# One more buffer for queries and keys, nine weight pieces and another order of mish ahead of an attention and mixture-of-experts kernel

## The chip, the cores and the metric

The kernel runs on one core of a Trainium2 chip. The time is device time in microseconds (us) of one execution; three executions of the kernel before took 829.11, 832.15 and 832.38 us, so the median is 832.15. One further execution was profiled; all rows of this document that show the kernel before come from it.

The core has TensorE (PE in the rows; PEld is its loading of weights), VectorE (DVE), ScalarE (ACT) and GpSimd (POOL). SP and ScalarE each have a queue from which they start DMA transfers (SPq, ACTq).

## The reference

Three parts follow one another on 2304 tokens:

```python
# attention: q, k, v are [4, 8, 576, 64]; heads 0-3 window 32, heads 4-7 window 128 with step 4
attn = softmax(where(mask, q @ k.T / 8, -1e9));  x = attn @ v        # x: [2304, 512]
# dense layer with mish
h = x @ w_in                                                        # [2304, 2048]
x = (h * tanh(softplus(h))) @ w_out                                  # [2304, 512]
# eight experts, one per token
e = argmax(x @ w_gate);  p = softmax(x @ w_gate)[e];  s = sigmoid(x @ w_output_gate)[e]
out = p * s * (relu(x @ w1[e]) @ w2[e])                              # w1: 512x1024, w2: 1024x512
```

## The kernel before

**Halves and tasks.** The tokens are worked in NH = 8 half-batches j of 288 tokens. The attention of a half-batch is four tasks (j, p), each a pair of heads: p = 0, 1 have the plain window, p = 2, 3 the dilated one. `load(j, p)` (line 202) brings what a task needs, queries, keys and values side by side, in one transfer into one tile `qkv` (992 or 1216 columns; line 213). Tasks of j = 0, 1 load on SP into memory that weights take later. The tasks from j = 2 on load on ScalarE's queue and share two buffers, so the load of task t + 2 can start when the last reader of task t, its product with the values (`o`, line 315), is done. A task is then: scores (`sc`, line 251), a row maximum on VectorE, exponentials on ScalarE (line 278), a division by the sums, transposes (`tp`, line 295) and the product `o`, which is split into two parts `xhi`, `xlo` (lines 325, 328).

**The dense layer.** Every product runs in three passes over a high and a low part of both factors (high times high, high times low, low times high). A step g of the main loop handles 128 of the 2048 hidden columns for one half-batch: `l1` (line 494) makes `hps` with 12 matmuls; mish is computed in place in a tile `e` by steps a to d; `l2` (line 547) adds its product with `w_out` to `acc`, three steps later. The steps of mish are: a1 an exponential on ScalarE that reads `hps` (line 502), a2 a minimum and an addition on VectorE (line 505), a3 a square on ScalarE (line 510), b a logarithm and an exponential on ScalarE (lines 522, 523), c a product with `hps` on VectorE (line 528), d the split into `ghi` on ScalarE (line 417) and `glo` on VectorE (line 418). `hps` has two buffers, so `l1` of step g + 2 has to wait for c of step g.

**Weights.** The weights of the dense layer come in 32 pieces of 128 x 512 values, alternately of `w_in` and `w_out`. SP loads a piece into a staging tile `wst`; it is narrowed to the bits that a matmul uses in two steps (`upper`, line 401 on ScalarE or 403 on VectorE, then `wf`, line 407 on VectorE) and split into a high part on ScalarE (line 448 or 417) and a low part on VectorE (line 453 or 418).

**Order.** `ahead` is the front of the program: in it the order on TensorE, ScalarE, VectorE and SP is as written. Its iterations t carry one task of j = 0, 1 each in a pipeline (scores of t + 1, exponentials of t, transposes and `o` of t - 1, split of t - 2); beside it the first seven pieces (`wide_first`, line 163) are narrowed, cast on ScalarE, and the first four `l1` steps with their mish are run. After `ahead` a scheduler orders by priority. The main loop calls l1, mish and l2 and spreads the attention of the next half-batch over its steps; `att_d` of a task (its `o`) is followed by `next_load`, the load of the task two further on.

**The end.** The experts run one after another on rows gathered by expert. The outputs of the last expert are two row tiles; each goes through ScalarE or, for every second tile, half through VectorE and half through ScalarE, and is then scattered to `out` by an indirect DMA of GpSimd (line 908). A count of tokens that didn't fit (`rest_count`) is read into a register of every engine, and a loop `rest` runs that often, which is zero times for these inputs.

Of the kernel before, what the change touches and what calls it, by code (L numbers as in the profile page):

```python
# [9 lines left out]
F32 = mybir.dt.float32  # L10
# [13 lines left out]
DIL = 4  # L24
# [7 lines left out]
def tile_attn_mish_moe(ctx, tc, qkv, w_in, w_out, w_gate, w_og, w1, w2, out):  # L32
# [108 lines left out]

    def setup_rows(e):
        if not fills:
            fills.append(mp.tile([128, ROW], F32, tag="fill", name="fill", bufs=1))
            nc.vector.memset(fills[0], 0.0)
            nc.gpsimd.iota(fills[0].bitcast(I32)[:, DM + 1:DM + 2], pattern=[[0, 1]], base=OOB, channel_multiplier=1)
        for i in range(0, MOST, 128 * (MOST // 128)):
            n = min(128 * (MOST // 128), MOST - i)
            k, m = max(1, n // 128), min(n, 128)
            tc.keep_in_program_order(nc.sync.dma_start(  # L150
                out=buf[e * NT + i:e * NT + i + n, :].rearrange("(i p) c -> p i c", p=m),
                in_=fills[0][0:m].unsqueeze(1).to_broadcast([m, k, ROW])))
# [7 lines left out]
        xlo[j] = xp.tile([128, KD, HS], F32R, tag="xlo", name="xlo")  # L160

    EARLY = 2
    wide_first = 7
    STEPS = 4
    LAG = 3
    AHEAD = 3
# [38 lines left out]
    def load(j, p):  # L205

        n = 992 if p < 2 else 1216
        if j < 2 and p:
            off = 992 + 1216 * (p - 2) if p > 1 else 0
            t = scq[j][:, off:off + n]  # L210
        else:
            t = raw.tile([128, 1216], F32, tag="qkv", name="qkv", bufs=2)[:, 0:n]
        (nc.sync if j < 2 else nc.scalar).dma_start(out=t, in_=qkv[j, p, :, 0:n])
        kv = t[:, HS:]
        if p < 2:
            kT, vr = kv[:, 0:HS + 32], kv[:, HS + 32:].rearrange("p (u h d) -> p u h d", u=3, h=2)
        else:
            kT = kv[:, 0:HS + 4 * 32].rearrange("d (c p) -> d c p", c=DIL)
            vr = kv[:, HS + 4 * 32:].rearrange("p (h c d) -> p h c d", h=2, c=DIL)
        state[j, p] = dict(qT=t[:, 0:HS], kT=kT, v=vr)  # L220

    def form(j, p):
        return (3, CH, 128) if p < 2 else (DIL, NP, NP + 32 * (j % 2))
# [129 lines left out]
    def next_load():  # L353
        if n_l[0] < len(tasks):
            load(*tasks[n_l[0]])
            n_l[0] += 1

    def attention(j):

        ops = []  # L360
        for p in range(5):
            if p < 4:
                ops.append(lambda p=p: att_s(j, p))
            if p > 0:
                ops.append(lambda p=p: att_c(j, p - 1))
                ops.append(lambda p=p: (att_d(j, p - 1), next_load()))
        return ops


# [498 lines left out]
    def e_l2_end(q, part):  # L868

        for t, (i, m) in enumerate(part):  # L870
            for f in (NF2 - 2, NF2 - 1):
                for n, (a, x) in enumerate(PASS):
                    nc.tensor.matmul(out=accs["e", q][t], lhsT=gt["e", q, f][x][:, i:i + m],
                                     rhs=ew[q, 1, a][:, DM * f:DM * f + DM], start=False, stop=(f == NF2 - 1 and n == 2))
            e_row(q, i, m, accs["e", q][t], t)

    def e_l2(q, f, part):

        gg = gt.pop(("e", q, f))
# [18 lines left out]
    def e_row(q, i, m, src, alt=0):  # L898

        x = meta[q, 0][0:m, i // 128, :]  # L900
        o = rp.tile([128, DM], F32, tag="row", name="eo")
        if alt % 2:

            nc.vector.tensor_scalar(out=o[0:m, 0:DM // 2], in0=src[:, 0:DM // 2], scalar1=x[:, 0:1], scalar2=None, op0=ALU.mult)
            nc.scalar.activation(out=o[0:m, DM // 2:], in_=src[:, DM // 2:], func=AF.Copy, scale=x[:, 0:1])
        else:
            nc.scalar.activation(out=o[0:m], in_=src, func=AF.Copy, scale=x[:, 0:1])
# [27 lines left out]
    def rest_count():  # L935
# [21 lines left out]
        return cnt, rem, nc.values_load(tn[0:1, 0:1], min_val=0, max_val=NT // 128 + E)  # L957

    def rest(cnt, rem, n):

# [65 lines left out]
    def ahead(load_w, warm):  # L1026
# [12 lines left out]
            a_max(*t, 0)  # L1039
            a_max(*t, 1)  # L1040
        last = None
        for t in range(len(T) + 2):
            now = T[t] if t < len(T) else None
            old = T[t - 1] if 0 < t <= len(T) else None
            old2 = T[t - 2] if 1 < t else None
            new = T[t + 1] if 0 < t < len(T) - 1 else None
            w, w2 = t - 1, t - 2
            g, g1, g2 = t - ends, t - ends - 1, t - ends - 2
            is_ = lambda i, n: 0 <= i < n

            load_w()
            if t < 4:
                next_load()

            if old2:
                a_hi(*old2)
            if is_(g1, STEPS):
                mish_a1(g1)
            if old:
                a_norm(*old)  # L1060
            if is_(g1, STEPS):
                mish_a2(g1)
            if now:
                a_exp(*now, 0)
            if is_(g1, STEPS):
                mish_a3(g1)
            if old:
                a_turn(*old, 0)
                a_turn(*old, 1)
            if old2:  # L1070
                a_lo(*old2)
            if is_(w2, wide_first):
                w_lo(w2)
                nw[1] += 1
            if old:
                a_copy(*old, 0)
            if now:
                a_exp(*now, 1)
            if old:
                a_copy(*old, 1)  # L1080
            if is_(g1, STEPS):
                mish_b(g1)
            if new:
                a_scores(*new)
            if is_(w, wide_first):
                w_b(w)
            if new:
                a_alloc(*new)
                a_max(*new, 0, False)
                a_max(*new, 1, "both")  # L1090
            if old:
                a_out(*old)
            if is_(g1, STEPS):
# [15 lines left out]
    if True:  # L1109
# [131 lines left out]
    if True:  # L1241
# [23 lines left out]
        for q in range(1, E):  # L1265
# [5 lines left out]
            for f in range(NF2 + 1):  # L1271
                if f < NF2:
                    e_l1(q, f, CAPS[q], exh[q], exl[q], mg, (("egh", EGB), ("egl", EGB)))
                    e_splits_to(8 * (q + 1) + f + 1)
                if f >= 1 and (q < E - 1 or f < NF2 - 1):
                    e_l2(q, f - 1, tiles(q))
                if outs and f >= 1:
                    outs.pop(0)()
# [1 line left out]
                    ops.pop(0)()  # L1280
            while ops:
                ops.pop(0)()
            if q < E - 1:
                outs = e_out(q, tiles(q))
                if q == E - 2:
                    left = rest_count()
            else:
# [64 lines left out]
```

## Time and profile before

| what | us |
|---|---|
| median of three runs (lowest, highest) | 832.15 (829.11, 832.38) |
| the profiled execution, its own time | 831.06 |
| its span, first to last instruction | 829.3 |
| TensorE busy | 790.9 |
| VectorE busy | 544.0 |
| ScalarE busy | 502.8 |

Every time in a row is counted from the start of the span. A row of the timeline gives start, duration, engine, line, operation, `out<-in`, shapes, and in brackets the idle time of that engine just before with what ended it. The chain of waits is the sequence of work that ended last, followed back from the last instruction. [...]

### The profile page before, as it was taken

To read this page: it belongs to the slowest core of one execution; us is meant where nothing else is said; L and a number is where in the kernel's file an instruction comes from. 1 tells how busy PE (TensorE), PEld (TensorE's weight loads), DVE (VectorE), ACT (ScalarE), POOL (GpSimd) and SP (SyncE) were. 2 spreads that over 40 slices of the span, in tenths; PEclk is the share of its full clock that TensorE was granted. 3 is DMA by queue.
4 is the path that set the end of the run, shared out by engine and by line. 5 is a ranking of instruction groups with operands and counts; after the bars stand their busy time and mean duration, and the time that the engine had idled before them with its cause. 6 is when DMAs were issued, how large, how long until landed. Compare 5 with 4: busy or idle time off the path is not lost.

```text
span 829.3 us, 16404 instructions
## 1 busy us (share of the span) xinstructions
PE 790.9 (95%) x6125; PEld 739.0 (89%) x6125; DVE 544.0 (66%) x1459; ACT 502.8 (61%) x1426; POOL 53.3 (6%) x88
## 2 busy tenths in 40 slices
PE   7789997999999999999999999999999999999994
PEld 5579996998999999999999899999899989999983
DVE  6869896887757757867767766784682635644710
ACT  5978875875667657667666665582661644644611
POOL 1000000001100100100100000101110111001100
PEclk9999997999999999999999999999999999999997
DMA  9837743101110210211111010431873627536300
GB/s 347 261 104 265 220 149 107 56 26 60 61 50 31 61 50 31 61 50 32 51 35 45 26 46 2 157 102 30 299 257 110 216 76 243 176 114 228 127 24 19
DMA packets 39596, 91.27 MB, mean 110 GB/s; under 512 B 4591, under 2 KB 12783, under 8 KB 39515
## 3 DMA queue, kind: packets, MB, share of 16 engines
q1 hardware_dynamic: 32811, 67.18, 24.8%
q10 hardware_dynamic: 3456, 13.57, 5.2%
q0 software_dynamic: 3248, 9.46, 3.3%
q8 instruction: 49, 0.80, 0.4%
q14 instruction: 32, 0.26, 0.1%
HBM read 73.77 MB, written 17.00 MB: 109 GB/s over the span
## 4 chain that ended last, share of the span: by engine, by line
PE 69%; DVE 10%; issue 7%; DMA 6%; ACT 5%; POOL 1%; SPq 1%; POOLq 0%; ACTq 0%; DVEq 0%
PE hps L494 21%; PE acc L547 20%; PE eh L842 8%; PE ecol L886 6%; PE eacc L894 3%; PE o L315 3%; PE sc L251 2%; DMA est<-in_moe_w_dram 2%; DMA qkv<-in_qkv_dram 1%; ACT pr L278 1%; PE tp L295 1%; ACT scr L278 1%; DVE pr L266 1%; PE rows L671 1%; DMA wst<-in_moe_w_in_dram 1%
## 5 line engine op out<-in xcount | busy, mean ns | idle before, releaser
L494 PE MATMUL hps<-xhi,w 128*128 128x288 f32 x1024 | 236.2, 304 | 5.1 <-DVE e L528 4.9
L494 PEld LDWEIGHTS hps<-xhi,w 128*128 128x128 f32 x1024 | 174.3, 190 | 10.4 <-DVE e L528 6.9
L547 PE MATMUL acc<-ghi,w 128*128 128x288 f32 x1024 | 171.9, 303 | 1.9 <-DVE x2T L565 1.4
L494 PE MATMUL hps<-xlo,w 128*128 128x288 f32 x512 | 153.1, 299 | 0.1
L547 PEld LDWEIGHTS acc<-ghi,w 128*128 128x128 f32 x1024 | 146.0, 190 | 7.4 <-DVE x2T L565 2.3
L842 PE MATMUL eh<-exh,we 128*128 128x424 f32 (+6 forms) x448 | 106.0, 311 | 0.0
L418 DVE TENSOR_TENSOR we<-est,we 128x512 fp32r<-128x512 f32 x128 | 83.0, 685 | 27.9 <-ACT we L417 27.5
L494 PEld LDWEIGHTS hps<-xlo,w 128*128 128x128 f32 x512 | 97.4, 190 | 1.4 <-DVE xlo L328 1.3
L417 ACT ACTIVATE we<-est 128x512 fp32r<-128x512 f32 x128 | 74.7, 624 | 34.0 <-DMA est<-in_moe_w_dram 17.9
L547 PE MATMUL acc<-glo,w 128*128 128x288 f32 x512 | 92.0, 296 | 0.0
L502 ACT ACTIVATE e<-hps 128x288 f32<-128x288 f32 x128 | 51.8, 405 | 62.9 <-PE hps L494 62.6
L522 ACT ACTIVATE e<-e,two 128x288 f32<-128x288 f32 x128 | 67.9, 531 | 33.1 <-DVE e L512 32.3
L842 PEld LDWEIGHTS eh<-exh,we 128*128 128x128 f32 x448 | 76.6, 189 | 1.2
L547 PEld LDWEIGHTS acc<-glo,w 128*128 128x128 f32 x512 | 76.5, 189 | 0.0
L417 ACT ACTIVATE ghi<-e 128x288 fp32r<-128x288 f32 x128 | 56.1, 438 | 32.9 <-PE acc L547 24.9
L418 DVE TENSOR_TENSOR glo<-e,ghi 128x288 fp32r<-128x288 f32 x128 | 58.1, 454 | 26.0 <-ACT ghi L417 15.4
L278 ACT ACTIVATE pr<-pr,nm 96x128 f32<-96x128 f32 (+2 forms) x168 | 62.0, 370 | 15.1 <-DVE nm L267 14.6
L842 PE MATMUL eh<-exl,we 128*128 128x424 f32 (+6 forms) x224 | 68.8, 307 | 0.0
L528 DVE SCALAR_TENSOR_TENSOR e<-e,hps 128x288 f32<-128x288 f32 x128 | 57.4, 448 | 16.8 <-ACT e L523 16.5
L847 DVE SCALAR_TENSOR_TENSOR eg<-eh,eg 128x256 fp32r<-128x256 f32 (+6 forms) x64 | 30.4, 476 | 57.6 <-ACT eg L846 57.4
L505 DVE TENSOR_SCALAR e<-e 128x288 f32<-128x288 f32 x128 | 39.0, 305 | 44.2 <-ACT e L502 43.9
L886 PE MATMUL ecol<-eg,we 128*128 128x424 f32 (+3 forms) x384 | 63.8, 317 | 0.0
(197 smaller groups left out, 1196.1 us busy)
## 6 DMA issues: line engine op xcount, KB each, us to landing
est<-in_moe_w_dram SPq DMA_DIRECT2D x64, 512.0 KB, 5.2
wst<-in_moe_w_in_dram SPq DMA_DIRECT2D x16, 512.0 KB, 10.8
wst<-in_moe_w_out_dram SPq DMA_DIRECT2D x16, 512.0 KB, 4.3
qkv<-in_qkv_dram ACTq DMA_DIRECT2D x12, 608.0 KB, 5.0
buf<-fill SPq DMA_DIRECT2D x8, 771.0 KB, 7.6
qkv<-in_qkv_dram ACTq DMA_DIRECT2D x12, 496.0 KB
xs<-buf SPq DMA_DIRECT2D x17, 257.0 KB, 4.0
scq<-in_qkv_dram SPq DMA_DIRECT2D x4, 608.0 KB
```

The lines of the kernel that those rows point to most:

```text
L278: nc.scalar.activation(out=st["p"][:, h, u, :], in_=src[:, u, :], func=AF.Exp, bias=st["nm"][0:m, h, u:u + 1], scale=scale, accum_out=st[" ...
L417: nc.scalar.activation(out=hi, in_=src, func=AF.Copy)
L418: return nc.vector.tensor_tensor(out=lo, in0=src, in1=hi.bitcast(F32), op=ALU.subtract)
L494: mm = nc.tensor.matmul(out=hps[g], lhsT=w[:, a, kk, 128 * fl:128 * fl + 128], rhs=(xhi, xlo)[x][j][:, kk, :], start=(kk == 0 and n == 0), ...
L502: nc.scalar.activation(out=e, in_=hps[g], func=AF.Exp)
L505: nc.vector.tensor_scalar(out=mt[g], in0=mt[g], scalar1=math.exp(20.0), scalar2=1.0, op0=ALU.min, op1=ALU.add)
L522: nc.scalar.activation(out=r, in_=r, func=AF.Ln, scale=0.2, bias=two5)
L528: nc.vector.scalar_tensor_tensor(out=u, in0=u, scalar=2.5, in1=hps.pop(g), op0=ALU.subtract, op1=ALU.mult)
L547: nc.tensor.matmul(out=accs[j][m], lhsT=w[:, a, fl, 128 * m:128 * m + 128], rhs=gg[x], start=(first and n == 0), stop=(last and n == 2))
L842: nc.tensor.matmul(out=ps, lhsT=ew[q, 0, a][:, c:c + 128], rhs=(hi, lo)[x][:, kk, 0:n], start=(k == 0), stop=(k == 3 * KD - 1))
L847: nc.vector.scalar_tensor_tensor(out=gl, in0=ps, scalar=0.0, in1=gh.bitcast(F32), op0=ALU.max, op1=ALU.subtract)
L886: nc.tensor.matmul(out=accs["e", q][k], lhsT=ew[q, 1, a][:, c:c + 128], rhs=gg[x], start=(f == 0 and n == 0), stop=(f == NF2 - 1 and n == 2))
```

## The change

1. **Loads.** The tile `qkv` becomes two: `qk` with queries and keys (608 or 704 columns, three buffers) and `v` with the values (384 or 512 columns, two buffers). `load_on`, called behind `att_d` of task t, issues `v` of task t + 2 and `qk` of task t + 3. After `ahead`, `qk` of task (2,2) is issued as well, the third in its buffers.
2. **The fill tile** that clears rows for the experts is now a slice of a staging buffer (`wst2`); its memset stands earlier.
3. **`wide_first`** goes from 7 to 9: the pieces 7 and 8 are narrowed in `ahead`.
4. **mish in `ahead`.** a1 stands behind the first exponentials of the task, a2 behind the low part of a piece, a3 behind the second copy, c behind the high part of a piece; d is done one iteration later, so the loop of iterations is one longer.
5. **The last expert** ends like the others, each row tile through ScalarE alone.
6. **The count** is computed before the last outputs of the expert before the last and read into the registers behind the last scatter.

```diff
@@ load
+            if what != "v":
+                qk = raw.tile([128, 704], F32, tag="qk", name="qk", bufs=3)[:, 0:n1]
+                (nc.sync if j < 2 else nc.scalar).dma_start(out=qk, in_=qkv[j, p, :, 0:n1])
+                state[j, p] = dict(qk=qk)
+            if what != "qk":
+                v = raw.tile([128, 512], F32, tag="v", name="v", bufs=2)[:, 0:n - n1]
+                (nc.sync if j < 2 else nc.scalar).dma_start(out=v, in_=qkv[j, p, :, n1:n])
...
+    def load_on(t):
+
+        if t + 2 < len(tasks):
+            load(*tasks[t + 2], "v")
+        if t + 3 < len(tasks):
+            load(*tasks[t + 3], "qk")
...
-                ops.append(lambda p=p: (att_d(j, p - 1), next_load()))
+                ops.append(lambda p=p: (att_d(j, p - 1), load_on(4 * j + p - 1)))
@@ setup_rows
-            fills.append(mp.tile([128, ROW], F32, tag="fill", name="fill", bufs=1))
+            fills.append(wst2[:, 3 * 1032:3 * 1032 + ROW])
@@ numbers
-    wide_first = 7
+    wide_first = 9
@@ ahead
-        for t in range(len(T) + 2):
+        for t in range(len(T) + 3):
...
             if old2:
                 a_hi(*old2)
-            if is_(g1, STEPS):
-                mish_a1(g1)
             if old:
                 a_norm(*old)
-            if is_(g1, STEPS):
-                mish_a2(g1)
             if now:
                 a_exp(*now, 0)
             if is_(g1, STEPS):
-                mish_a3(g1)
+                mish_a1(g1)
...
+            if is_(g1, STEPS):
+                mish_a2(g1)
+            if is_(g2, STEPS):
+                last = mish_d(g2).ins
...
             if is_(g1, STEPS):
+                mish_a3(g1)
                 mish_b(g1)
...
+            if is_(w, wide_first):
+                w_hi(w)
             if is_(g1, STEPS):
                 mish_c(g1)
-            if is_(w, wide_first):
-                w_hi(w)
             if is_(t, wide_first):
                 w_a(t)
-            if is_(g1, STEPS):
-                last = mish_d(g1).ins
@@ behind ahead
         for _ in range(2):
             next_load()
+        load(*tasks[n_l[0]], "qk")
@@ the last expert
-                if q == E - 2:
-                    left = rest_count()
-            else:
-                e_l2_end(q, tiles(q))
-    rest(*left)
+        with tc.manual_schedule(engines={ET.Pool}):
+            e_out(E - 1, tiles(E - 1))
+            n = nc.values_load(left[2][0:1, 0:1], min_val=0, max_val=NT // 128 + E)
+    rest(*left[:2], n)
```

**ScalarE in the front.** The rows are those of one iteration of `ahead` with a step of the dense layer beside a task; `scr` are the exponentials of the task, `e` the tile of mish, `w<-wf` the high part of a piece, `upper` its cast. The first fence is the kernel before, the second the changed one, whose line numbers are its own (502 is now 519, 278 is 288, 510 is 527, 417 is 434).

```order
L502 ACTIVATE e<-hps 128x288
L278 ACTIVATE scr,su<-sc,nm 72x104 x4
L510 ACTIVATE e<-e 128x288
L278 ACTIVATE scr,su<-sc,nm 72x104 x4
L304 ACTIVATE scr<-tp 104x288
L522 ACTIVATE e<-e,two_109 128x288
L523 ACTIVATE e<-e 128x288
L448 ACTIVATE w<-wf 128x512
L417 ACTIVATE ghi<-e 128x288
```

```order
L288 ACTIVATE scr,su<-sc,nm 72x104 x4
L519 ACTIVATE e<-hps 128x288
L434 ACTIVATE ghi<-e 128x288
L288 ACTIVATE scr,su<-sc,nm 72x104 x4
L314 ACTIVATE scr<-tp 104x288
L527 ACTIVATE e<-e 128x288
L539 ACTIVATE e<-e,two_109 128x288
L540 ACTIVATE e<-e 128x288
L465 ACTIVATE w<-wf 128x512
L418 ACTIVATE upper<-wst 128x512
```

The first Exp of mish moved behind the first four exponentials, the square from between the exponentials to directly ahead of the logarithm, and the `ghi` that stands here is that of the step before; a cast of a later piece is behind the high part, where there was none.

**VectorE around the end of the front.** The rows are those at the first steps behind the tasks; `upper` and `wf` are the narrowing of a piece, `w<-wf,w` its low part.

```order
L528 SCALAR_TENSOR_TENSOR e<-e,hps 128x288
L418 TENSOR_TENSOR glo<-e,ghi 128x288
L505 TENSOR_SCALAR e<-e 128x288
L403 CAST upper<-wst 128x512
L407 SCALAR_TENSOR_TENSOR wf<-wst,upper 128x512
L403 CAST upper<-wst 128x512
L505 TENSOR_SCALAR e<-e 128x288
L407 SCALAR_TENSOR_TENSOR wf<-wst,upper 128x512
L528 SCALAR_TENSOR_TENSOR e<-e,hps 128x288
L418 TENSOR_TENSOR w<-wf,w 128x4x128
```

```order
L545 SCALAR_TENSOR_TENSOR e<-e,hps 128x288
L338 TENSOR_TENSOR xlo<-o,xhi 128x4x72
L470 TENSOR_TENSOR w<-wf,w 128x4x128
L522 TENSOR_SCALAR e<-e 128x288
L435 TENSOR_TENSOR glo<-e,ghi 128x288
L424 SCALAR_TENSOR_TENSOR wf<-wst,upper 128x512
L522 TENSOR_SCALAR e<-e 128x288
L545 SCALAR_TENSOR_TENSOR e<-e,hps 128x288
L470 TENSOR_TENSOR w<-wf,w 128x512
```

Between two products (528, now 545) stood two casts and two `wf`; now one `wf` stands there and the casts of these pieces are ScalarE's.

**ScalarE's queue in the main loop.** The rows are those at the first loads of the main loop: before, the load of task (2,2); now the `qk` of the tasks behind it and the first `v`. `pr` are exponentials of a task.

```order
L417 ACTIVATE ghi<-e 128x288
L522 ACTIVATE e<-e,two_109 128x288
L213 DMA qkv<-in_qkv_dram 128x1216
L523 ACTIVATE e<-e 128x288
L502 ACTIVATE e<-hps 128x288
```

```order
L527 ACTIVATE e<-e 128x288
L216 DMA qk<-in_qkv_dram 128x704
L434 ACTIVATE ghi<-e 128x288
L539 ACTIVATE e<-e,two_109 128x288
L288 ACTIVATE pr,su<-pr,nm 96x128 x6
L540 ACTIVATE e<-e 128x288
L216 DMA qk<-in_qkv_dram 128x608
L519 ACTIVATE e<-hps 128x288
```

The load of (2,2) was an issue between the logarithm and the exponential of a step. Its `qk` no longer stands here: it has moved into `ahead`, between a cast (`upper`) and a split (`xhi`). What stands here instead are issues for later tasks, two for each task where there was one.

## Rows read from the trace of the kernel before

**Rows 1.** Page, whole span: engine, busy us, share, instructions.
```profile
PE 790.9 (95%) x6125; PEld 739.0 (89%) x6125; DVE 544.0 (66%) x1459; ACT 502.8 (61%) x1426; POOL 53.3 (6%) x88
```
**Rows 2.** Busy us by stretch: stretch, length, engines, TensorE clock, DMA share.
```profile
33.00:40.00 7.00, 4.82 (x49) 3.77 (x50) 5.66 (x14) 6.20 (x26) 0.00 (x0) 1.00 0.62 179
40.00:67.00 27.00, 23.93 (x173) 22.10 (x174) 17.66 (x40) 19.25 (x56) 0.00 (x0) 0.87 0.36 119
67.00:115.00 48.00, 48.00 (x364) 47.95 (x363) 45.02 (x105) 39.87 (x94) 0.00 (x0) 1.00 0.74 239
115.00:128.00 13.00, 12.37 (x99) 10.98 (x97) 12.55 (x32) 9.52 (x37) 0.00 (x0) 1.00 0.28 83
128.00:146.00 18.00, 13.26 (x80) 11.99 (x80) 9.09 (x21) 9.19 (x32) 0.00 (x0) 0.72 0.37 122
146.00:165.00 19.00, 19.00 (x180) 17.42 (x178) 15.81 (x43) 15.24 (x51) 0.00 (x0) 1.00 0.20 61
...
200.00:530.00 330.00, 326.18 (x2734) 308.01 (x2731) 233.35 (x713) 215.04 (x671) 16.78 (x18) 1.00 0.14 41
```
**Rows 3.** Timeline of TensorE, 131 to 137 us: start, us, instruction, idle before.
```profile
131.93 0.40 PE L494 MATMUL hps<-xhi,w 128*128 128x288 f32 x1 [1.25 <-DVE e L528]
...
136.35 1.20 PE L251 MATMUL sc<-qkv 64*72 64x72 f32 x8 [3.49 <-DMA qkv<-in_qkv_dram]
```
**Rows 4.** Timeline of ScalarE and its queue, 128 to 130 us.
```profile
128.91 0.33 ACTq L213 DMA_DIRECT2D qkv<-in_qkv_dram  x1
129.30 0.45 ACT L523 ACTIVATE e<-e 128x288 f32<-128x288 f32 x1 [0.63 <-PE o L315]
```
**Rows 5.** Timeline of the SP queue, 128 to 134 us.
```profile
128.62 4.43 SPq L389 DMA_DIRECT2D wst<-in_moe_w_out_dram  x2
```
**Rows 6.** Chain of waits, 128 to 137 us: start, us, what.
```profile
128.91 7.30 DMA qkv<-in_qkv_dram
```
**Rows 7.** Busy us by stretch around that wait.
```profile
131.00:136.00 5.00, 0.93 (x5) 0.70 (x5) 2.21 (x5) 2.58 (x6) 0.00 (x0) 0.85 0.88 303
136.00:145.00 9.00, 8.65 (x43) 8.13 (x44) 4.77 (x12) 3.99 (x19) 0.00 (x0) 0.51 0.02 10
```
**Rows 8.** Chain of waits, 34 to 42 us.
```profile
34.77 0.41 ACT e L502
35.18 1.30 ACT scr L278 x8
...
36.81 1.31 ACT scr L278 x8
...
39.35 0.46 DVE e L528
...
39.85 1.87 PE hps L494 x12
```
**Rows 9.** Chain of waits, 58 to 67 us.
```profile
59.16 0.70 DVE wf L407
...
61.55 2.23 PE hps L494 x12
63.78 2.75 PE acc L547 x12
```
**Rows 10.** Timeline of TensorE, 61 us.
```profile
61.55 0.40 PE L494 MATMUL hps<-xhi,w 128*128 128x288 f32 x1 [1.74 <-DVE e L528]
```
**Rows 11.** Chain of waits, 88 us.
```profile
88.79 1.59 PE hps L494 x12
```
**Rows 12.** Timeline of TensorE, the later waits for an attention load.
```profile
199.22 0.94 PE L251 MATMUL sc<-qkv 64*72 64x104 f32 x16 [1.28 <-DMA qkv<-in_qkv_dram]
...
458.79 0.40 PE L251 MATMUL sc<-qkv 64*72 64x104 f32 x4 [0.80 <-DMA qkv<-in_qkv_dram]
```
**Rows 13.** Tile qkv, issues on ScalarE's queue: min/median/max ns, first and last start.
```profile
L213 ACTq DMA_DIRECT2D qkv<-in_qkv_dram x24: 334/334/419, 14.6 to 476.2; - x24
```
**Rows 14.** Timeline of GpSimd, the end of the program.
```profile
818.54 1.03 POOL L908 DMA_INDIRECT out_dram<-eo,meta  x1 [0.52 <-ACTq L965]
```

More of the change, by code (lines that the diff above doesn't have):

```diff
@@ L203, in fill, with load @@
             nc.tensor.matmul(out=spare[0], lhsT=idb, rhs=idb[:, 0:96], start=False, stop=True, skip_group_check=True)
-    def load(j, p):
-        n = 992 if p < 2 else 1216
+    def load(j, p, what="all"):
+        n, n1 = (992, 608) if p < 2 else (1216, 704)
         if j < 2 and p:
@@ L210, in load @@
             t = scq[j][:, off:off + n]
-        else:
-            t = raw.tile([128, 1216], F32, tag="qkv", name="qkv", bufs=2)[:, 0:n]
-        (nc.sync if j < 2 else nc.scalar).dma_start(out=t, in_=qkv[j, p, :, 0:n])
-        kv = t[:, HS:]
+            nc.sync.dma_start(out=t, in_=qkv[j, p, :, 0:n])
+            qk, v = t[:, 0:n1], t[:, n1:]
+        else:
+            if what != "v":
[5 more added lines that the diff above has]
+                (nc.sync if j < 2 else nc.scalar).dma_start(out=v, in_=qkv[j, p, :, n1:n])
+                qk = state[j, p]["qk"]
+            if what == "qk":
+                return
+        kT = qk[:, HS:]
         if p < 2:
-            kT, vr = kv[:, 0:HS + 32], kv[:, HS + 32:].rearrange("p (u h d) -> p u h d", u=3, h=2)
+            vr = v.rearrange("p (u h d) -> p u h d", u=3, h=2)
         else:
-            kT = kv[:, 0:HS + 4 * 32].rearrange("d (c p) -> d c p", c=DIL)
-            vr = kv[:, HS + 4 * 32:].rearrange("p (h c d) -> p h c d", h=2, c=DIL)
-        state[j, p] = dict(qT=t[:, 0:HS], kT=kT, v=vr)
+            kT = kT.rearrange("d (c p) -> d c p", c=DIL)
+            vr = v.rearrange("p (h c d) -> p h c d", h=2, c=DIL)
+        state[j, p] = dict(qT=qk[:, 0:HS], kT=kT, v=vr)
     def form(j, p):
@@ L866, in e_l1_late @@
         gt["e", 0, f] = (gh, gl)
[L868 to L875, printed above, removed]
     def e_l2(q, f, part):
@@ L896, in e_l2, with e_row @@
                                  start=(f == 0 and n == 0), stop=(f == NF2 - 1 and n == 2))
-    def e_row(q, i, m, src, alt=0):
+    def e_row(q, i, m, src):
         x = meta[q, 0][0:m, i // 128, :]
         o = rp.tile([128, DM], F32, tag="row", name="eo")
-        if alt % 2:
-            nc.vector.tensor_scalar(out=o[0:m, 0:DM // 2], in0=src[:, 0:DM // 2], scalar1=x[:, 0:1], scalar2=None, op0=ALU.mult)
-            nc.scalar.activation(out=o[0:m, DM // 2:], in_=src[:, DM // 2:], func=AF.Copy, scale=x[:, 0:1])
-        else:
-            nc.scalar.activation(out=o[0:m], in_=src, func=AF.Copy, scale=x[:, 0:1])
+        nc.scalar.activation(out=o[0:m], in_=src, func=AF.Copy, scale=x[:, 0:1])
         ins = nc.gpsimd.indirect_dma_start(
@@ L956, in rest_count @@
         nc.vector.tensor_copy(tn, tf)
-        return cnt, rem, nc.values_load(tn[0:1, 0:1], min_val=0, max_val=NT // 128 + E)
+        return cnt, rem, tn
     def rest(cnt, rem, n):
@@ L1041, in ahead @@
         last = None
-        for t in range(len(T) + 2):
+        for t in range(len(T) + 3):
             now = T[t] if t < len(T) else None
             old = T[t - 1] if 0 < t <= len(T) else None
-            old2 = T[t - 2] if 1 < t else None
+            old2 = T[t - 2] if 1 < t < len(T) + 2 else None
             new = T[t + 1] if 0 < t < len(T) - 1 else None
@@ L1274, in tile_attn_mish_moe @@
                     e_splits_to(8 * (q + 1) + f + 1)
-                if f >= 1 and (q < E - 1 or f < NF2 - 1):
+                if f >= 1:
                     e_l2(q, f - 1, tiles(q))
@@ L1282, in tile_attn_mish_moe @@
                 ops.pop(0)()
+            if q == E - 2:
+                left = rest_count()
             if q < E - 1:
                 outs = e_out(q, tiles(q))
-                if q == E - 2:
-                    left = rest_count()
-            else:
-                e_l2_end(q, tiles(q))
-    rest(*left)
+        with tc.manual_schedule(engines={ET.Pool}):
+            e_out(E - 1, tiles(E - 1))
+            n = nc.values_load(left[2][0:1, 0:1], min_val=0, max_val=NT // 128 + E)
+    rest(*left[:2], n)
 _INS = ['qkv', 'moe_w_in', 'moe_w_out', 'moe2_w_gate', 'moe2_w_output_gate', 'moe2_w1', 'moe2_w2']
```

## The prediction, on record before the changed kernel ran

> **What bounds the kernel now.** I read the page's busy line first. TensorE works 790.9 us of the span of 829.3 and VectorE 544.0 [rows 1], so the kernel is bound by TensorE, and a change can win only where TensorE stands idle or where its clock is lowered. The second view is a table by stretch [rows 2]. From 67 to 115 us TensorE is busy for all of 48.00 us at full clock, and from 200 to 530 for 326.18 of 330.00. Three places are left. The front, 33 to 40: TensorE works 4.82 of 7.00 while ScalarE works 6.20, so ScalarE sets the pace. The next stretch, 40 to 67: TensorE works 23.93 of 27.00 at a mean clock of 0.87. And 128 to 146: 13.26 of 18.00, clock 0.72.
>
> The third view is the timeline of TensorE in that last place. It waits 1.25 us for VectorE at 131.93 and 3.49 us for an attention load at 136.35 [rows 3]. [...] Together the hole costs 1.25 + 3.49 + 4.4 = 9.1 us.
>
> Why the load comes late is read from ScalarE's queue. The issue stands at 128.91, and the instruction behind it waited 0.63 us for TensorE's `o` [rows 4]: the product that was the last reader of the buffer to be filled. The transfer then takes 7.30 us on the chain [rows 6], beside two weight pieces that SP started at 128.62 [rows 5]; from 131 to 136 the DMA engines are busy for 0.88 of the time, and from 136 to 145 for 0.02 [rows 7]. So this load waited for a buffer, not for its queue's turn, and then met the weights.
>
> **The change, part by part.** *Queries and keys in three buffers.* The load of task (2,2) (half-batch 2, head pair 2) no longer needs the buffer of (2,0): its queries and keys go out from the hand-ordered front, long before 128 us, and its values, which `o` needs only after scores, softmax and transposes, keep two buffers. The 3.49 go, and with them the reason for the low clock. What is late next is VectorE: of its 1.25 us of wait I leave half, 0.6, since less transfer competes with the pieces that it converts. For the rest of the stretch I leave the idle rate of the stretch ahead of it, (13.00 − 12.37)/13.00 × 18 = 0.9 [rows 2]. So 9.1 − 0.6 − 0.9 = 7.6 us are won. Bounds: 9.1 if nothing is left; 3.5 if only the load's own wait goes and the clock falls all the same.
>
> Two later waits have the same releaser, 1.28 at 199.22 and 0.80 at 458.79 [rows 12]. The 24 issues stand between 14.6 and 476.2 us [rows 13]; all but the first two stand in the main loop, from 128.91 on, so 21 steps of (476.2 − 128.9)/21 = 16.5 us in the mean, and a buffer more brings the queries and keys forward by about one such step, far over either wait. I take both off: 2.1 (bounds 0 and 2.1).
>
> Against this stand 24 more issues on ScalarE's queue at 334 ns [rows 13], 8.0 us of queue time. If all of it reached TensorE it would cost 8.0. In 200 to 530 ScalarE is busy 215.04 of 330.00, and TensorE idles only 3.82 there [rows 2]; by the share 3.82/215.04 the cost would be 0.1. I take 1.1, near the lower end, because ScalarE has a third of its time free to absorb an issue.
>
> *Another order of mish in the front.* In one turn of the front the chain now runs through everything: hps 1.87, Exp 0.41 at 34.77, four score exponentials (1.30), the square, four more (1.31 from 36.81), and so on to VectorE's product (0.46 at 39.35), which frees the next hps at 39.85 [rows 8]. One turn is 39.85 − (34.77 − 1.87) = 6.95 us. After the change the split into ghi and glo stands an iteration later, the first Exp behind the first exponentials, and the product behind ScalarE's conversion of a weight piece. The two-buffered hps is still freed by the product, so the loop remains, but ScalarE's queue is not held by steps that wait for VectorE. No turn can be shorter than ScalarE's work, so 7.00 − 6.20 = 0.8 us is the most for each; two turns have scores beside a step, 1.6 in all. The extra iteration adds no instruction to TensorE.
>
> *Nine pieces instead of seven.* Pieces 7 and 8 are now narrowed by ScalarE in the front, not by VectorE beside the first steps of the loop. There TensorE waits 1.74 us for VectorE's product [rows 10], and the chain ahead of it is VectorE's conversion, 0.70 for one `wf` [rows 9]. With two casts and two `wf` out of the way I leave the product itself, 0.46 [rows 8]: 1.3 us are won. Behind the wait one run of hps takes 2.23 us and one of acc 2.75 [rows 9], against 1.59 for hps at 88.79 [rows 11], so the clock is low after it. The whole stretch loses 27.00 × (1 − 0.87) = 3.5 to the clock and 3.07 to idle [rows 2]. Of that idle 0.8 + 1.3 go, two thirds, which would return 2.4; I take half of it, 1.2, as I can't tell which wait lowered the clock. The front sums to 1.6 + 1.3 + 1.2 = 4.1. Bounds: 0, since work moved to ScalarE may hold what it freed, and 0.8 + 3.07 + 3.5 = 7.4.
>
> *The rest.* The fill tile's memset goes into the front, where VectorE has 1.3 of 7.00 us free [rows 2]: nothing, at most one 128-partition write like the 0.70. At the end the last expert's two row tiles come one after the other from ScalarE, and the count is read behind the last scatter. The second scatter starts at 818.54, 0.52 after what released it, and takes 1.03 [rows 14]. The first tile finishes earlier and the second waits for GpSimd behind it: a gain of at most 0.5, a loss of at most 1.0, taken at nothing as both are near it.
>
> **Sum.** −4.1 − 7.6 − 2.1 + 1.1 = −12.7 against the profiled execution of 831.06 us gives 818.4. The median shown, 832.15, lies 1.1 above that execution, so I forecast 819.5.
>
> **The rivals.** B: the front gives nothing. ScalarE works 6.20 of 7.00 there already and takes over two more casts; against it speaks that from 54 us on it is no longer full (19.25 of 27.00 in the stretch [rows 2]). Time: 819.5 + 4.1 = 823.6.
>
> C: VectorE takes the load's place. From 115 to 165 it works 12.55 + 9.09 + 15.81 = 37.45 of 50 us [rows 2]; pressed into some 41 us that is 0.91. Then TensorE keeps waiting for converted pieces, the clock stays low, and the hole gives 3.5 only: 819.5 + 4.1 = 823.6. Against it: at 45.02 of 48.00, 0.94, TensorE lost nothing from 67 to 115. B and C together: 827.7.
>
> D, the slower side: ScalarE's queue blocked by its own issues. A queries-and-keys buffer is free only when TensorE has done that task's scores, and ScalarE can't pass a waiting issue. Each of the 21 such issues left in the main loop may then hold ScalarE for a run of scores, 0.94 to 1.20 us [rows 3, 12], and TensorE with it through hps. At 1.20 that is 25.2 − 13.8 (the gains) = 11.4 more than before: 831.06 + 11.4 + 1.1 = 843.6. It decides from 13.8/21 = 0.66 us for each issue. For it: the 0.63 of [rows 4] is just such a hold. Against it: with 115 of 330 us free, ScalarE can stand a hold of 0.66 in each 16.5 us unless the product is due at that moment.
>
> [...]
>
> E: the change does not do what it says. The hole stays whole because the pieces that SP brings are as late as the load was, and the front only gets longer: −2.1 + 1.1 = −1.0, or 831.2.
>
> **How the numbers follow.** The forecast has 0.60, B 0.14, C 0.09, B with C 0.05, D 0.05, E 0.07. About 0.5% (4.2 us) is what a measurement of this kernel can tell from no change. The range reaches down to the sum of all upper bounds, 831.06 − 7.4 − 9.1 − 2.1 + 0.1 + 1.1 = 813.7, rounded to 813.5, and up to 827.0, which covers B and C and leaves out B with C, D and E, 0.17. Faster: forecast, B, C and most of B with C, less a little for unseen costs, 0.86. E and the margin, 0.09, are no change; D, 0.05, is slower.
>
> **What would show it.** In the changed profile no instruction of TensorE should wait for queries and keys, and the wait of 3.49 should be gone with the clock at 1.00 in the 9 us behind its place. There should be no wait like 1.74 in the first loop steps, and two hps runs of the front should stand about 6.2 us apart, not 6.95. If waits for VectorE's `e` sum to over 3 us from 115 to 165, C holds; if ScalarE idles over 0.66 us behind most issues, D. I am wrong if the hole closes and the time does not fall by at least 4 us.

## The result and the profile after

The changed kernel took 818.92 us in the median (816.08 to 821.29, four runs) against 832.26 in four runs of the kernel before; the ratio is 0.9844, with an interval of 0.9801 to 0.9886. The forecast was 819.5 with a range of 813.5 to 827.0. Timed again in five further runs it took 817.97, ratio 0.984 (0.9827 to 0.9852). The profiled execution took 819.34 with a span of 817.6, 11.7 less than the span before.

The page's busy line of the changed kernel, the counterpart of [rows 1]: TensorE does the same 6125 matmuls in nearly the same time, in a shorter span.

```profile
PE 789.5 (97%) x6125; PEld 739.2 (90%) x6125; DVE 543.2 (66%) x1456; ACT 504.6 (62%) x1428; POOL 52.5 (6%) x88
```

The table by stretch of the changed kernel, with the columns of [rows 2]. Each row has the stretch, its length, the busy us of TensorE, weight loads, VectorE, ScalarE and GpSimd with their counts of instructions, TensorE's mean granted clock as a share of full speed, the mean busy share of the DMA engines, and GB/s:

```profile
33.00:40.00 7.00, 7.00 (x70) 5.88 (x69) 6.08 (x15) 5.85 (x27) 0.00 (x0) 0.76 0.58 179
40.00:67.00 27.00, 24.43 (x209) 22.48 (x206) 22.34 (x51) 24.51 (x71) 0.00 (x0) 1.00 0.54 180
67.00:115.00 48.00, 48.00 (x366) 47.69 (x365) 42.43 (x97) 37.52 (x90) 0.00 (x0) 1.00 0.67 210
115.00:128.00 13.00, 12.07 (x96) 10.56 (x97) 12.68 (x32) 10.18 (x39) 0.00 (x0) 1.00 0.47 135
128.00:146.00 18.00, 17.07 (x146) 15.57 (x145) 16.39 (x43) 15.11 (x53) 0.00 (x0) 1.00 0.51 152
146.00:165.00 19.00, 19.00 (x164) 17.83 (x164) 13.56 (x35) 14.68 (x42) 0.00 (x0) 1.00 0.09 25
200.00:530.00 330.00, 327.37 (x2741) 310.76 (x2740) 232.59 (x692) 218.28 (x664) 17.13 (x20) 1.00 0.17 48
```

Three things are to be seen. From 128 to 146 the clock is 1.00 and TensorE works 17.07 of 18.00; it was 0.72 and 13.26. From 40 to 67 the clock is 1.00 as well, and ScalarE works 24.51 us where it worked 19.25. But from 33 to 40 the clock is now 0.76, which the prediction did not foresee.

The timeline of TensorE in the changed kernel, the front and the place of the hole (answering [rows 3, 10]):

```profile
36.22 0.61 PE L511 MATMUL hps<-xhi,w 128*128 128x288 f32 x1
...
42.58 0.40 PE L511 MATMUL hps<-xhi,w 128*128 128x288 f32 x1 [1.15 <-DVE e L545]
...
48.92 0.40 PE L511 MATMUL hps<-xhi,w 128*128 128x288 f32 x1 [0.50 <-DVE e L545]
...
127.56 0.73 PE L261 MATMUL sc<-qk 64*72 64x72 f32 x8
...
130.28 0.73 PE L261 MATMUL sc<-qk 64*72 64x72 f32 x8
...
135.22 0.38 PE L325 MATMUL o<-pt,v 128*64 128x96 f32 x2 [0.53 <-ACT pt L314]
135.91 0.40 PE L511 MATMUL hps<-xhi,w 128*128 128x288 f32 x1 [0.32 <-DVE e L545]
```

The scores of (2,2) at 127.56 and 130.28 wait for nothing. What remains there is 0.53 us for ScalarE's transposed exponentials (`pt`) and 0.32 for VectorE's `e`. In the front the steps of the dense layer start at 36.22, 42.58 and 48.92, that is 6.36 and 6.34 apart; before it was 6.95, and about 6.2 was forecast. The wait of 1.74 us is gone.

ScalarE and its queue in the changed kernel (answering [rows 4]), and the 9 us behind the hole's place (answering [rows 7]):

```profile
116.61 0.34 ACTq L216 DMA_DIRECT2D qk<-in_qkv_dram  x1
...
127.07 0.33 ACTq L220 DMA_DIRECT2D v<-in_qkv_dram  x1
127.45 0.44 ACT L540 ACTIVATE e<-e 128x288 f32<-128x288 f32 x1 [0.86 <-PE o L325]
...
131.04 0.33 ACTq L216 DMA_DIRECT2D qk<-in_qkv_dram  x1
131.43 0.36 ACT L288 ACTIVATE pr<-pr,nm 72x72 f32<-72x72 f32 x1 [1.48 <-PE sc L261]
```

```profile
136.00:145.00 9.00, 8.91 (x80) 8.14 (x81) 8.78 (x23) 7.83 (x23) 0.00 (x0) 1.00 0.46 138
```

An issue of `qk` did hold ScalarE: the exponential behind the one at 131.04 waited 1.48 us for the scores. From 120 to 500 us that is the only idle time of ScalarE that its timeline puts down to scores; behind the 43 issues of the main loop, `v` included, ScalarE idles more than 0.66 us 8 times, mostly until a product of TensorE (`acc`). So the slower rival (a hold of more than 0.66 us at each of 21 issues) did not come about. Nor did the rival in which VectorE takes the load's place: from 115 to 165 TensorE waits 0.32 us for VectorE's `e` (and 0.92 for its `pr`, ahead of the hole's place), where the prediction's sign was 3 us for `e`.

**Where the time went, by stretches of work.** A stretch of the time axis holds other work in each kernel, so the traces are better compared between the same steps of the dense layer. Step g starts with the first of its twelve `hps` matmuls in the timeline of TensorE. In the kernel before steps 22 and 27 start at 114.12 and 148.36, in the changed one at 112.35 and 139.09. Times in us, each from one profiled execution; the kernels other than the first and the last two are the experiments below, and "front" says whose front a kernel has.

| profiled execution | front | start of step 0 | steps 0 to 22 | steps 22 to 27 (the hole) | step 27 to the end of the span |
|---|---|---|---|---|---|
| before | old | 32.88 | 81.24 | 34.24 | 680.9 |
| end alone | old | 35.81 | 80.26 | 34.31 | 680.1 |
| loads alone | old | 35.35 | 80.46 | 25.69 | 677.5 |
| order of mish alone | part new | 35.66 | 80.58 | 33.74 | 678.4 |
| nine pieces alone | part new | 33.71 | 80.32 | 31.94 | 680.3 |
| front alone | new | 33.74 | 76.15 | 31.96 | 681.4 |
| one tile | new | 38.96 | 76.49 | 31.52 | 680.2 |
| two buffers | new | 35.70 | 75.81 | 26.64 | 679.1 |
| 16 fillers | new | 36.29 | 75.46 | 26.26 | 678.9 |
| front's loads on SP | new | 36.01 | 76.36 | 26.39 | 680.1 |
| all loads on SP | new | 33.63 | 76.07 | 25.76 | 676.1 |
| all loads on SP, 16 fillers | new | 33.73 | 75.83 | 25.71 | 677.0 |
| changed | new | 36.22 | 76.13 | 26.74 | 678.5 |
| changed, once more | new | 34.73 | 75.92 | 26.87 | 679.4 |

The hole gives 34.24 − 26.74 = 7.5 us and steps 0 to 22 give 5.1; 3.3 are lost ahead of step 0, and from step 27 on 2.4 are won. The sum is 7.5 + 5.1 − 3.3 + 2.4 = 11.7.

### The profile page after: what moved, and what is told of

Its sections match the earlier page's. It is cut to its first block, busy times and chain, and to the rows that moved or that the text cites. A ratio compares the mean times of both kernels' runs of the same rounds, so it can differ in the third digit from the quotient of the medians.

```text
span 817.6 us, 16466 instructions
## 1 busy us (share of the span) xinstructions
PE 789.5 (97%) x6125; PEld 739.2 (90%) x6125; DVE 543.2 (66%) x1456; ACT 504.6 (62%) x1428; POOL 52.5 (6%) x88
## 4 chain that ended last, share of the span: by engine, by line
PE 72%; DVE 7%; issue 7%; ACT 6%; DMA 5%; POOL 1%; SPq 1%; POOLq 0%; ACTq 0%; DVEq 0%
PE hps L511 22%; PE acc L564 20%; PE eh L859 9%; PE ecol L894 6%; PE eacc L902 3%; PE o L325 2%; ACT pr L288 2%; DMA wst<-in_moe_w_in_dram 2%; PE sc L261 2%; DMA est<-in_moe_w_dram 1%; PE rows L688 1%; PE tp L305 1%; DMA qk<-in_qkv_dram 1%; PE eh L874 1%; PE lgT L614 1%
## 5 line engine op out<-in xcount | busy, mean ns | idle before, releaser
L539 ACT ACTIVATE e<-e,two 128x288 f32<-128x288 f32 x128 | 67.9, 530 | 26.8 <-DVE e L529 25.7
L564 PEld LDWEIGHTS acc<-glo,w 128*128 128x128 f32 x512 | 76.1, 188 | 0.1
```

The costliest lines, as they stand in the source:

```text
L539: nc.scalar.activation(out=r, in_=r, func=AF.Ln, scale=0.2, bias=two5)
L564: nc.tensor.matmul(out=accs[j][m], lhsT=w[:, a, fl, 128 * m:128 * m + 128], rhs=gg[x], start=(first and n == 0), stop=(last and n == 2))
```

## The experiments

### Loads alone, front alone

The first kernel is the one before with the edits 1 and 2 (loads, fill tile), the second the one before with 3 and 4 (nine pieces, order of mish).

> The kernel before with the loads alone: queries and keys in three buffers, values in two, the early load of task (2,2), and the fill tile moved to make room. Theory (loads and front act apart): the hole behind step 25 of the dense layer closes (wait for the load gone, clock 1.00), steps 0 to 8 stand where they stood; 832.3 - 7.0 - 1 = 824. Rival (the hole closes only because VectorE was relieved in the front): TensorE then waits for VectorE there and the time is 828 or more. Rival (loads give it all): 820.

Measured: 822.22 us, ratio 0.990 (0.9864 to 0.9935). The forecast by the theory, 824, is nearest; the interval, 819.3 to 825.2, takes in the 820 of the second rival as well, which the gain of the front alone, below, speaks against.

> The kernel before with the front alone: nine pieces and the other order of mish, loads as before. Theory: step 8 of the dense layer comes 4.1 us earlier, the load of (2,2) still waits for its buffer and the hole stays, 832.3 - 4.1 = 828. Rival (the front shifts the weight transfers away from the load so that the hole shrinks too): 824 or less. Rival (the earlier front only makes the wait in the hole longer): 831 or more.

Measured: 824.94 us, ratio 0.9917 (0.9886 to 0.9948). Of the times the first rival's came closest, and the hole shrank too. Step 8 starts at 65.83 us in its profile, 3.9 earlier than before (69.69), as the theory has it.

By ratio the loads give 8.3 us, the front 6.9, together 15.2, where both at once give 13.0. The difference is the part of the hole that either closes. In the loads-alone kernel, TensorE by stretch, and the wait that stood at 61.55 before [rows 10]:

```profile
40.00:67.00 27.00, 21.82 (x173) 19.90 (x174) 17.80 (x41) 20.07 (x59) 0.00 (x0) 0.94 0.38 123
128.00:146.00 18.00, 17.34 (x148) 15.52 (x148) 16.38 (x42) 14.38 (x47) 0.00 (x0) 1.00 0.43 136
```

```profile
64.47 0.40 PE L511 MATMUL hps<-xhi,w 128*128 128x288 f32 x1 [1.71 <-DVE e L545]
```

The hole's place runs at clock 1.00, while the wait at the end of the front stays, 1.71 us. So the hole closes without any relief of VectorE. In the front-alone kernel, TensorE around the hole and at the next load, and the stretch:

```profile
128.91 0.40 PE L494 MATMUL hps<-xhi,w 128*128 128x288 f32 x1 [1.78 <-DVE e L528]
...
130.40 0.71 PE L251 MATMUL sc<-qkv 64*72 64x72 f32 x8 [0.69 <-DMA qkv<-in_qkv_dram]
...
193.99 0.94 PE L251 MATMUL sc<-qkv 64*72 64x104 f32 x16 [2.56 <-DMA qkv<-in_qkv_dram]
```

```profile
128.00:146.00 18.00, 16.40 (x117) 15.26 (x119) 13.44 (x35) 11.30 (x38) 0.00 (x0) 0.81 0.35 117
```

The load costs 0.69 us of wait in place of 3.49, and the clock 0.81 in place of 0.72; the next load waits longer, 2.56 in place of 1.28 [rows 12]. The front alone shortens steps 22 to 27 by 34.24 − 31.96 = 2.3 us, nearly the 2.2 by which the two gains overlap. The nine pieces alone shorten them as much (31.94).

### Which part of the loads closes the hole

Two kernels take the changed one and undo a part. "Two buffers" takes the third buffer away, so each task's loads are issued behind `att_d` two tasks ahead as before:

```diff
-                qk = raw.tile([128, 704], F32, tag="qk", name="qk", bufs=3)[:, 0:n1]
+                qk = raw.tile([128, 704], F32, tag="qk", name="qk", bufs=2)[:, 0:n1]
...
-            load(*tasks[t + 2], "v")
-        if t + 3 < len(tasks):
-            load(*tasks[t + 3], "qk")
+            load(*tasks[t + 2])
...
-        load(*tasks[n_l[0]], "qk")
```

> The changed kernel with two buffers for queries and keys instead of three, so that each task's loads are issued two tasks ahead as before, still in two transfers. Theory (the third buffer closes the hole): the hole is back, 819 + 7 to 9 = 826 to 828. Rival (that queries and keys come free earlier, after the scores, and in a smaller transfer is enough): 820.

Measured: 819.79 us, ratio 0.9862 (0.9826 to 0.9897). The theory fell; the time is that of the changed kernel. ScalarE and its queue in this kernel, and TensorE at the scores of (2,2):

```profile
115.64 0.33 ACTq L216 DMA_DIRECT2D qk<-in_qkv_dram  x1
...
126.12 0.33 ACTq L220 DMA_DIRECT2D v<-in_qkv_dram  x1
126.50 0.44 ACT L538 ACTIVATE e<-e 128x288 f32<-128x288 f32 x1 [0.89 <-PE o L325]
```

```profile
126.61 0.73 PE L261 MATMUL sc<-qk 64*72 64x72 f32 x8
...
129.33 0.73 PE L261 MATMUL sc<-qk 64*72 64x72 f32 x8
```

With two buffers the `qk` of (2,2) is issued at 115.64, once the scores of (2,0) are done, 10.5 us ahead of the values at 126.12, which wait for `o`, and 11.0 ahead of the first use at 126.61. No third buffer is needed for that.

"One tile" goes one step further back: one transfer for queries and keys, one for the values, but into one tile `qkv` of two buffers again.

```diff
-                qk = raw.tile([128, 704], F32, tag="qk", name="qk", bufs=3)[:, 0:n1]
+                t = raw.tile([128, 1216], F32, tag="qkv", name="qkv", bufs=2)[:, 0:n]
+                qk = t[:, 0:n1]
...
-                v = raw.tile([128, 512], F32, tag="v", name="v", bufs=2)[:, 0:n - n1]
+                v = t[:, n1:]
```

> The changed kernel with queries, keys and values in one tile of two buffers again, still in two transfers, queries and keys first; the front is the changed one. Against the kernel with two buffers of their own for queries and keys it differs in one thing: the buffer's last reader is the product o again, not the scores. Theory (the earlier last reader closes the hole, not the third buffer and not the smaller transfer): the load of (2,2) is issued behind o again and the time is that of the front alone, 824 to 826. Rival (the smaller transfer alone is enough): 820.

Measured: 825.68 us, ratio 0.9934 (0.9908 to 0.9959), as the theory has it. ScalarE's queue, TensorE at the scores, and the stretch around them:

```profile
130.84 0.33 ACTq L217 DMA_DIRECT2D qkv<-in_qkv_dram  x1
131.22 0.45 ACT L539 ACTIVATE e<-e 128x288 f32<-128x288 f32 x1 [0.66 <-PE o L326]
131.25 0.46 ACTq L221 DMA_DIRECT2D qkv<-in_qkv_dram  x1
```

```profile
135.16 0.71 PE L262 MATMUL sc<-qkv 64*72 64x72 f32 x8 [1.48 <-DMA qkv<-in_qkv_dram]
```

```profile
131.00:146.00 15.00, 13.22 (x85) 11.75 (x84) 10.02 (x25) 9.33 (x32) 0.00 (x0) 0.77 0.45 144
```

The issue stands behind `o` again, at 130.84, the scores wait 1.48 us, and the clock falls to 0.77. So what closes the hole is that the buffer's last reader is now the scores and no longer `o`; the third buffer adds nothing that can be measured, and against the front alone the smaller transfer by itself is worth 31.96 − 31.52 = 0.4 us in the hole.

### The parts of the front

The kernel before with the order of mish alone, and with nine pieces alone (and the longer loop of iterations that the ninth needs):

> The kernel before with the other order of mish in the front alone (seven pieces, loads as before). Theory (the turn of the front is set by ScalarE's queue): steps 0 to 4 stand 1.6 us closer together, 832.3 - 1.6 = 830.7. Rival (order is the main part of the front's gain): 829 or less; rival (the later split of ghi costs what the order gives): 832.3.

Measured: 829.01 us, ratio 0.9966 (0.9943 to 0.9988): 2.8 us, nearer to the rival; the interval, 1.0 to 4.7 us, holds the 1.6 of the theory too.

> The kernel before with nine pieces in the front alone (one iteration more of the front, order of mish and loads as before). Theory: the wait of 1.74 us ahead of step 6 goes and part of the clock with it, 832.3 - 2.5 = 829.8. Rival (two more casts on ScalarE push the steps of the front back by what they save): 832.3 or more.

Measured: 827.95 us, ratio 0.9964 (0.9946 to 0.9982): 3.0 us; the forecast was 2.5. The two sum to 5.8, and both at once give 6.9, which the intervals don't set apart.

The traces say more. The order alone brings steps 0 and 4 closer together, from 23.2 to 23.8 us in the three profiles of the old front to 19.84. But behind them a wait of 2.03 us for the high part of a piece stands in its trace; in that of the nine pieces alone the wait ahead of step 6 is still 1.01 us, and steps 0 and 4 stand 24.37 apart. The two rows, in this order:

```profile
64.33 0.89 PE L547 MATMUL acc<-ghi,w 128*128 128x288 f32 x4 [2.03 <-ACT w L417]
```

```profile
64.39 0.40 PE L494 MATMUL hps<-xhi,w 128*128 128x288 f32 x1 [1.01 <-DVE e L528]
```

So in these profiles neither alone shortens steps 0 to 22 (80.58 and 80.32, old fronts 80.26 to 81.24); both together do, to 75.5 to 76.5, and neither wait is in the traces of the whole front.

### The end alone

The edits 5 and 6 on the kernel before:

> The kernel before with the end alone: the last expert's two row tiles through ScalarE, the count read last. Theory: no change, 832 (within 1). Rival (the register read held the end up): 830.5.

Measured: 830.93 us, ratio 0.9993 (0.9973 to 1.0014): no change. The end of the changed kernel, GpSimd (answering [rows 14]):

```profile
805.51 0.98 POOL L911 DMA_INDIRECT out_dram<-eo,meta  x1 [19.54 <-ACT eo L910]
806.79 1.03 POOL L911 DMA_INDIRECT out_dram<-eo,meta  x1 [0.30 <-issue]
```

The second scatter starts 1.28 us behind the first and no longer 1.5, as only GpSimd's own issue (0.30) lies between them, where a wait of 0.52 that ScalarE's queue ended stood before [rows 14]; a few tenths, as bounded.

### The clock ahead of step 0

The end-alone kernel shows something else. Its front is the old one, line for line, and step 0 starts 2.9 us later than in the profile before. Each fence is the stretch 10 to 20 us, first of the kernel before, then of the end-alone kernel:

```profile
10.00:20.00 10.00, 6.76 (x90) 5.34 (x91) 8.44 (x21) 8.59 (x36) 0.00 (x0) 0.92 1.05 396
```

```profile
10.00:20.00 10.00, 8.06 (x102) 6.62 (x99) 7.66 (x19) 8.95 (x42) 0.00 (x0) 0.70 1.04 396
```

The granted clock is 0.92 in the one and 0.70 in the other. So the clock that this stretch gets, and the start of step 0 with it, differ between executions of the same front. Over the fourteen profiles of the table the two go together: from 0 to 33 us the clock is 0.94 to 1.00 in the five whose step 0 starts by 33.74, 0.84 to 0.91 in seven that start it between 34.73 and 36.22, and 0.71 where it starts at 38.96. One falls out, the 16 fillers (0.94 and 36.29). Which of the two is the cause the profiles don't show. But the old front alone spreads over 2.9 us, and the second profile of the changed kernel starts step 0 at 34.73, so the 3.3 us that its first profile lost there can't be put down to the change. Could more filler matmuls (`fill`, whose result nothing reads) hold the clock up?

```diff
-                fill(10)
+                fill(16)
```

> The changed kernel with 16 filler matmuls instead of 10 in each iteration of the front that has no step of the dense layer. In the profile of the changed kernel the clock is 0.50 to 0.54 from 15 to 24 us and step 0 starts at 36.2, 3.3 us later than before. Theory (the low clock there delays the front): with the clock up, step 0 starts at 33 to 34 and the time is 816 to 817. Rival (the front up to step 0 is bound by the transfers and by ScalarE, and the clock does not matter): 819; rival (the fillers themselves delay it): 821.

Measured: 819.4 us, ratio 0.9854 (0.9831 to 0.9877). In its profile the clock from 0 to 33 us is 0.94, where it was 0.84 in the changed kernel, and yet step 0 starts at 36.29. The theory fell, and the fillers neither help nor harm.

### The price of the issues, and a faster kernel

> The changed kernel with the attention loads of the main loop issued on SP's queue instead of ScalarE's. Theory (48 issues of 334 ns on ScalarE cost next to nothing on the path): 819, within 1. Rival (the issues hold ScalarE up, as the slower rival of the prediction has it, only with a smaller price): 815 to 817. Rival (SP's queue, which also brings weight pieces, is held up by issues that wait for a buffer): 822 or more.

```diff
-                (nc.sync if j < 2 else nc.scalar).dma_start(out=qk, in_=qkv[j, p, :, 0:n1])
+                nc.sync.dma_start(out=qk, in_=qkv[j, p, :, 0:n1])
...
-                (nc.sync if j < 2 else nc.scalar).dma_start(out=v, in_=qkv[j, p, :, n1:n])
+                nc.sync.dma_start(out=v, in_=qkv[j, p, :, n1:n])
```

Measured: 814.69 us, ratio 0.9821 (0.9791 to 0.9852): the first rival, a small price on ScalarE. The edit moves all 48 loads, the five that stand in the front among them. Its interval reaches into that of the changed kernel, so three kernels ran side by side on one chip.

> The changed kernel with its attention loads on SP's queue and 16 filler matmuls instead of 10 in the front, to beat both kernels. Theory (the loads on SP save some 4 us, the fillers change nothing that can be measured): 815. Rival (what SP's queue gained was a kind clock in the front): 819. Rival (both add up): 812.

> The changed kernel with only the first five loads, those that stand in the front ((2,0), (2,1) and the queries and keys of (2,2)), on SP's queue, the others on ScalarE's. Theory (ScalarE sets the pace of the front, so an issue there costs, while the main loop hides it): 815 to 816. Rival (the gain of SP's queue is in the main loop): 818 to 819.

> The changed kernel as it is, once more, beside the others on the same chip: 819 (within 1). If it is 816 or less, the gain of SP's queue was none.

Measured: with SP's queue and 16 fillers 815.77 us, ratio 0.9807 (0.9787 to 0.9826); with only the front's five loads on SP 818.75, 0.9847 (0.9834 to 0.986); the changed kernel 817.97, 0.984 (0.9827 to 0.9852). The theory that the front's issues cost something fell: moving those alone gives nothing. Moving all gives 0.984 − 0.9807 = 0.0033 of 831.81, or 2.7 us; the two intervals just miss each other. As the fillers alone did nothing, and the front's five loads nothing, it is the main loop's issues that cost, together 2 to 4 us. The table shows where: with all loads on SP's queue steps 22 to 27 take 25.8 and 25.7 us, against 26.7 and 26.9 in the two profiles of the changed kernel, and step 27 to the end 676.1 and 677.0, against 678.5 and 679.4; steps 0 to 22 take the same. Whether the cost is the 334 ns of each issue or ScalarE standing behind an issue that waits for its buffer, as at 131.04, no run sets apart.

## Why the prediction was right, and where it was not

**The hole** was priced at 7.6 us and gave 7.5. That the load waited for a buffer and not for the queue is shown by the two-buffer and one-tile kernels, which differ in the buffer's last reader alone (819.79 and 825.68 us). The 4.4 us of clock in the 9.1 were an estimate, and no run shows them as a time of their own: TensorE was busy for 8.65 of the 9.00 us at a clock of 0.51 [rows 7], in the changed kernel for 8.91 at 1.00, and what the runs showed for wait and clock together is the 7.5 us of steps 22 to 27. The low clock goes with the wait: it stands behind the wait where the scores of (2,2) wait (3.49, 1.48 and 0.69 us, with a clock of 0.72, 0.77 and 0.81 in the stretches shown), and the loads alone take both away. But the step "queries and keys in three buffers ... go out from the hand-ordered front" named the wrong part. It is true that the load goes out there; but that it leaves so early is not what is needed. Two buffers do as well, because the scores of (2,0) free theirs 10.5 us ahead of `o` (issues at 115.64 and 126.12). The prediction read that `o` had released the issue and that only the values wait for `o`, but it credited the third buffer with what the split alone does. For VectorE, of whose wait 0.6 us were left, TensorE waits 0.32 (the row at 135.91).

**The front** was put at 4.1 us. The work from step 0 to step 22 became 5.1 shorter between the profiles of before and after. Over several profiles the old front takes 80.7 us in the mean of three (before, end alone, loads alone) and the new one 76.1 in the mean of five (front alone, one tile, two buffers, and the changed kernel twice): 4.6. Against that stands a step 0 that starts 34.7 us in on the old front and 35.9 on the new, so 3.4 net, a difference that the scatter ahead of step 0 could make or unmake. The size was right. That the spans differ by 11.7 us, near the 12.7 of the sum, is partly luck: between the two profiles the front and the stretch behind the hole gave 1.0 and 1.4 more than the sum has, and the delay ahead of step 0, which it does not have, took 3.3.

The mechanism "No turn can be shorter than ScalarE's work" is borne out by the turns of 6.36 and 6.34: in the second ScalarE is busy for 6.28 us (first row below, fourth engine). The chain of waits in the changed kernel stays on ScalarE from 38.65 to 48.39, over more than a turn, with gaps of 0.02 us. Its first part, from the Exp of a step to the cast of a piece, is the second block:

```profile
42.58:48.92 6.34, 5.33 (x48) 4.62 (x48) 4.44 (x11) 6.28 (x26) 0.00 (x0) 1.00 0.66 223
```

```profile
38.65 0.41 ACT e L519
39.06 1.30 ACT scr L288 x8
40.36 0.30 ACT scr L314
40.66 0.34 ACT e L527
...
41.02 0.54 ACT e L539
...
41.59 0.44 ACT e L540
42.03 0.52 ACT w L465
42.55 0.68 ACT upper L418
```

The sharing between order and pieces (1.6 and 1.3, besides the clock) is not borne out. Alone they give 2.8 and 3.0 us of time, clock included, but steps 0 to 22 get shorter only with both. The order's term was too small where it acts (3.4 to 3.9 us between steps 0 and 4, and not 1.6), and most of it is lost again behind step 4 as long as the pieces 7 and 8 are not narrowed in the front.

**The later loads and the added issues** were −2.1 and +1.1, together −1.0. No attention load is waited for any more, and from step 27 to the end the two profiles of the changed kernel are 2.4 and 1.5 us shorter than that of the kernel before. In the mean of the five profiles with the loads as before this part takes 680.2 us, in the mean of the six with the loads split into two tiles and the main loop's issues on ScalarE's queue 678.9: 1.3 us, near the forecast, though the two groups overlap (678.4 to 681.4, and 677.5 to 680.1). New in the changed kernel are waits of TensorE for the transposed exponentials `pt` that ScalarE copies. One of them, and the sum over the whole span from the view of that tile (who waited, us, times):

```profile
247.31 0.71 PE L325 MATMUL o<-pt,v 128*64 128x96 f32 x10 [0.48 <-ACT pt L314]
```

```profile
PE o L325: 2.0, 4
```

In the kernel before, in the one-tile kernel and in both kernels with all loads on SP's queue `o` has no such wait in that view, so these waits come with the split tiles on ScalarE's queue and not with the number of issues alone. What the issues cost is put at 2.7 us for all 48 by the kernel with SP's queue and 16 fillers, which is 1.4 for the 24 that were added, if they cost alike. That is an estimate; the prediction had taken 1.1.

**The end** was put at nothing, and the end alone measures as nothing. **The rivals**: the front gave something, VectorE did not take the load's place, one issue in the main loop held ScalarE for a run of scores and not 21, and the hole did not move elsewhere.

## What to carry to other kernels

When a transfer waits for its buffer, look at which reader frees it last and whether that reader needs the whole tile: a tile split by last reader can bring the early part in without a byte of extra buffering, and another buffer may then be worth nothing (here 819.79 us with two buffers for queries and keys, 818.92 with three). Two fixes for one stall don't add up (here 15.2 against 13.0), and two changes can need each other (here the order and the pieces), so time each alone before pricing both. And compare two traces between the same steps of work, with a second profile of unchanged code beside them, before a stretch is called won or lost.

## What the runs showed of the hardware

- The same front got different clocks in different executions: 0.92 and 0.70 from 10 to 20 us, and step 0 started between 32.88 and 35.81 us in the three profiles with the old front, between 33.63 and 38.96 in the nine with the new one. In the kernel with SP's queue and 16 fillers the same stretch ran at a clock of 1.00, with about as many matmuls as the kernel before had there (88 and 90) and fewer busy microseconds of TensorE (5.84 and 6.76):

```profile
10.00:20.00 10.00, 5.84 (x88) 4.62 (x88) 8.13 (x22) 8.08 (x36) 0.13 (x1) 1.00 1.05 395
```

- The DMA issues on ScalarE's queue cost time on the path, though ScalarE is busy for only 62% of the span: moving the 48 issues of 334 ns from ScalarE's queue to SP's (beside 16 fillers) took about 2.7 us off, a ratio of 0.9807 against 0.984.
